# Bias stage of an attention-plus-mixing kernel: written issue order on SyncE, and the last bias stores moved behind the first head pair's tile loads

## The chip, the cores and the metric

The kernel runs on one core of one Trainium2 chip. The metric is the device time of one execution in microseconds (us). Before the change it was 751.64 us (median of 3 runs, 751.6 to 753.61).

## What is computed

The reference is attention with a learned relative-position bias, followed by a Fourier mixing and a dense layer. Only the attention matters here (4 batches, 8 heads, 576 positions, head width 64, 32 hidden units in the bias network):

```python
rel = (pos[:, None] - pos[None, :])
x = (log1p(abs(rel)) / log1p(maximum(pos[:, None], 1.0)))[..., None]
h = maximum(x @ w1 + b1, 0.0)
bias = h @ w2                                   # 576 x 576 x 8 heads
scores = q @ k.T / 8 + bias.transpose(2, 0, 1)
attn = softmax(scores); out = attn @ v
```

The bias does not depend on the batch. It is computed once, for all 8 heads, and then used by 16 units (4 head pairs by 4 batches).

## The kernel before

**Two stages matter.** The bias stage computes the bias of all heads, in 36 groups `u` of 16 query rows, 4 steps each (144 steps `n`). Each step makes one hidden tile on VectorE (DVE) or ScalarE (ACT), lines 390 and 392 (three of four on DVE), and two matmuls on TensorE (PE), line 412. When a group is done, `bias_evac` copies its PSUM tile to a ring of 4 slots of 4 groups each (line 358, ACT). The attention stage then goes through the 16 units; every unit has nine blocks of scores: S (matmuls, line 282), D (bias added and row maximum, DVE, line 303), X (exponential, ACT, line 318), then transposes T and products with v.

**Where the bias goes.** With every fourth group (`u` = 3, 7, ... 35) a ring slot is full: 64 query rows of 8 heads. Two transfers take heads 0 and 1 from the ring straight into the first head pair's bias tiles in SBUF (line 367; for `u` = 35 three transfers of `rest_bias`, lines 257 to 260). Two such slots fill one tile: `u` = 27 and 31 fill the fourth. Six more transfers, `keep_bias` (line 351), store heads 2 to 7 of the slot in a DRAM buffer `bias_d`, from which `load_bias` (line 249) fetches the tiles of the later head pairs. That is 54 stores, of 144 KB each, in nine groups of six. All of these, and the loads of q and k (line 199) and v (line 206), are issued on SyncE's queue (SP). The q and k of a unit are then split into high and low parts by `prep`: units 0 and 1 on ACT (line 217) and DVE (line 223), the later ones on GpSimd (POOL, lines 219 and 223).

**Some blocks of unit 0 run early.** When a tile of the first pair is complete, `first_scores` issues S, D and X of unit 0 for it. Block 6 of unit 0 (here called D6) is the first to use the fourth tile; it is written after the loop over the steps. The bias stage has one PSUM tile for such scores, so the next block of unit 0 (S7) has to wait for D6. The attention stage follows in the order that the list `SECOND` gives: `S1 S7' D1 D7' X7' S2 T00' ...` (a prime stands for unit 0, none for unit 1).

**What sets the order.** Inside a block of `manual_schedule` the named engines issue in written order. Everywhere else a planner sets the order when the program is built: on a simulated timeline every free engine takes, of the instructions that are ready, the one written first. In the attention stage PE, DVE and ACT are in such a block and SP is not; in the bias stage no engine is. So a store, or a load that is written much later, may stand on SP's queue wherever the planner found the queue free. On the chip each queue then works in the order given, and an issue that waits holds up all behind it.

Of the kernel before, what the change touches and what calls it, by code (L numbers as in the profile page):

```python
# [9 lines left out]
F32 = mybir.dt.float32  # L10
# [8 lines left out]
B, H, S, D = 4, 8, 576, 64  # L19
DM, FF, HID = 512, 2048, 32  # L20
P = 128
HP = H // 2
CH = S // 2
# [4 lines left out]
L0, L1, L2 = 0, 42, 64  # L28
WAIT = 24
EV = 40  # L30
AHEAD = 19
HB = {"d": 8, "a": 6}
WHO = "ddda"
# [104 lines left out]
def body(ctx, tc, a, out):  # L138
    nc = tc.nc
# [53 lines left out]
    def load(n):  # L193
        hp, b = units[n]
        t = []
        for nm, w in (("qT", 2 * S), ("kT", KW)):
            f = ldp.tile([P, w], F32, tag=nm, name=nm)
            for e in range(2):
                nc.sync.dma_start(f[64 * e:64 * e + 64], a[nm][hp, b])
            t.append(f)  # L200
        ld[n] = t

    def load_v(n):
        hp, b = units[n]
        v = vt[n] = vp.tile([P, 5, P], F32, tag="v", name="v")
        nc.sync.dma_start(v, a["v"][hp, b].rearrange("(t p) c -> p t c", p=P))

    def prep(n):
        q, k = ld.pop(n)
        qs = stp.tile([P, 2 * S], F32R, tag="qs", name="qs")  # L210
        kh = stp.tile([P, KW], F32R, tag="kh", name="kh")
        kl = stp.tile([P, KW], F32R, tag="kl", name="kl")
        stk[n] = (qs, kh, kl)

        def hi(dst, src, c):
            if n < 2:
                nc.scalar.activation(dst[:, c], src[:, c], AF.Copy)
            else:
                nc.gpsimd.tensor_scalar(dst[:, c], src[:, c], 1.0, 0.0, ALU.mult, ALU.add)  # L219

        def lo(dst, src, ref, rows, c):
            eng = nc.vector if n < 2 else nc.gpsimd
            eng.tensor_tensor(dst[rows, c], src[rows, c], ref[rows, c].bitcast(F32), ALU.subtract)  # L223

        every, low = slice(0, 128), slice(64, 128)
        ca, cb, ck = slice(0, S), slice(S, 2 * S), slice(S, KW)
        return [
            lambda: hi(qs, q, ca), lambda: lo(qs, q, qs, low, ca),
            lambda: hi(kh, k, ca), lambda: lo(kl, k, kh, every, ca),
            lambda: hi(qs, q, cb), lambda: lo(qs, q, qs, low, cb),  # L230
            lambda: hi(kh, k, ck), lambda: lo(kl, k, kh, every, ck),
        ]
# [82 lines left out]
    def expo(n, i):  # L315
        blk = (BLK if n else BLK0)[i]
        p = prob(n, blk)
        nc.scalar.activation(  # L318
            p, p, AF.Exp, bias=nms[n][:, blk:blk + 1], scale=-1.0, accum_out=sums[n][:, blk:blk + 1])

    def first_scores(i):
        scores(0, i)
        largest(0, i)
        expo(0, i)

    with ExitStack() as st:
        hpool = pool("hp", 1, stack=st)
        ring = xp.tile([P, 4, 4, S], F32, tag="x", name="ring")
        bps = pool("bps", 3, PSUM, stack=st)
        sps = pool("sps0", 1, PSUM, stack=st)  # L330

        sm = rawp.tile([P, 66 + 5 * NG], F32, tag="raw", name="sm")
        w1c, b1c, w2 = sm[:, 0:1], sm[:, 1:2], sm[:, 2:66].rearrange("p (r c) -> p r c", r=2)
        lt, inv = sm[:, 66:66 + 4 * NG], sm[:, 66 + 4 * NG:]
        nc.sync.dma_start(sm, a["sm"])
        parts = ((512, 1148), (0, 512), (1148, NT0 + S))
        for i, (c0, c1) in enumerate(parts):
            (nc.sync if i else nc.scalar).dma_start(tw[:, c0:c1], a["tab"][:, c0:c1])
        nc.scalar.activation(sqp.tile([P, 8], F32, tag="sq", name="first")[:, 0:1], ident[:, 0:1], AF.Relu)
        nc.vector.tensor_scalar(lt, lt, b1c, None, ALU.mult)  # L340
        for i, (c0, c1) in enumerate(parts):
            if i == 9:
                nc.scalar.activation(tw[:, c0:c1], tw[:, c0:c1], AF.Copy, scale=w1c)
            else:
                nc.vector.tensor_scalar(tw[:, c0:c1], tw[:, c0:c1], w1c, None, ALU.mult)

        def keep_bias():

            u, src = later.pop(0)
            for e in range(2, H):  # L350
                nc.sync.dma_start(bias_d[4 * (u - 3):4 * (u + 1), e], src[:, e])  # L351

        def bias_evac(u, ps):
            g = u % 4
            o = ring[:, u // 4 % 4]
            dst = o[:, g].rearrange("p (c s) -> p c s", c=2)
            if u % EV != EV - 1:
                nc.scalar.activation(dst, ps[:, :, :CH], AF.Copy, scale=inv[:, u:u + 1])
            else:
                nc.vector.tensor_scalar(dst, ps[:, :, :CH], inv[:, u:u + 1], None, ALU.mult)  # L360
            if g < 3:
                return
            r0 = 16 * (u - 3)
            src = o.rearrange("(r h) g s -> r h g s", h=H)
            for e in range(2):
                if r0 < 512:
                    nc.sync.dma_start(bt[0, r0 // 128][r0 % 128:r0 % 128 + 64, e], src[:, e])
                else:
                    rest_bias(bt[0, 4], e, src[:, e])
            later.append((u, src))  # L370
            if len(later) > 1:
                keep_bias()
            if u % 8 == 7:
                due.extend([(4 * u + WAIT, u // 8 * 2), (4 * u + WAIT + 2, u // 8 * 2 + 1)])

        pending, early, later = [], [], []
        due = []
        ps = None
        steps = bias_steps()
        ahead = {}  # L380

        def hidden(n):
            u, t4, _, low, _ = steps[n]
            col = lt[:, 4 * u + t4:4 * u + t4 + 1]
            off = NT0 if low is None else N0 - low
            src = tw[:, off:off + S]
            who = WHO[n % len(WHO)]
            h = hpool.tile([P, S], F32, tag="h" + who, name="h" + who, bufs=HB[who])
            if who == "a":
                nc.scalar.activation(h, src, AF.Relu, bias=col)  # L390
            else:
                nc.vector.tensor_scalar(h, src, col, 0.0, ALU.add, ALU.max)  # L392
            return h

        for n, (u, t4, rev, low, _) in enumerate(steps):
            for k in range(n, min(n + AHEAD, len(steps))):
                if k not in ahead and (k <= n + 2 or WHO[k % len(WHO)] != "d"):
                    ahead[k] = hidden(k)
            if n in (L0, L1):
                load(n // L1)  # L400
                load_v(n // L1)
            if n in (L0, L2):
                early.extend(prep(n // L2))
            if early and n % 2:
                early.pop(0)()
            while due and due[0][0] <= n:
                first_scores(due.pop(0)[1])
            h = ahead[n]
            if t4 == 0:
                ps = bps.tile([P, 2, 512], F32, tag="ps", name="bps")  # L410
            for c in range(2):
                nc.tensor.matmul(  # L412
                    ps[32 * t4:32 * t4 + 32, c, :CH], w2[:, int(rev)], h[:, c * CH:(c + 1) * CH],
                    start=True, stop=True, tile_position=(0, 32 * t4),
                )
            if t4 == 3:
                pending.append((u, ps))
            if t4 == 2 and len(pending) > 1:
                bias_evac(*pending.pop(0))
        for e in pending:  # L420
            bias_evac(*e)
        for _, i in due[:-1]:
            first_scores(i)


    with ExitStack() as st:
# [161 lines left out]
        for n in range(U - 1):  # L588
            pr = prep(n + 1) if n else []
            if n in WIDE:  # L590
                wd = weights(WIDE.index(n))
            between = {4 + 8 * i: [piece] for i, piece in enumerate(pr)}
            turn_of(n, between)
            if n + 2 < U:
                load(n + 2)
            if n == 0:
                while later:
                    keep_bias()
                x = xp.tile([P, B, 5, DM], F32, tag="x", name="x")
            if n == 14:  # L600
                fs = tabp.tile([P, 3, 2, 2, NK], F32R, tag="tab", name="fs")
                nc.gpsimd.tensor_copy(fs[0:1, 0, 0, 0, 0:1], vt[14][0:1, 0, 0:1])
                nc.gpsimd.dma_start(fs, a["fs"])
# [215 lines left out]
        n = U - 1  # L819
# [4 lines left out]
        ut, across, high, low = flip(un)  # L824
# [77 lines left out]
        for w in TAIL:  # L902
            u = n - w.count("'")
# [604 lines left out]
```

## Time and profile before

| what | value |
|---|---|
| median of 3 runs | 751.64 us |
| the profiled execution's own time | 752.28 us |
| its span, first to last instruction | 750.5 us |
| PE busy | 734.4 us (98% of the span), 4731 instructions |
| DVE / ACT / POOL busy | 489.1 / 442.0 / 346.8 us |
| DMA queue of SP and its share of 16 engines | 58976 packets, 102.13 MB, 48.1% |
| stores bias_d<-ring | 54 of 144.0 KB, 2.8 us from issue to landing (median) |

The profiled execution is 0.64 us above the median of the runs; 1.78 us of its time lie outside the span. A row of a timeline gives the start, the duration, the engine, the line, the operation and its tiles, the count, and in brackets the idle time of the engine before it with the event that ended it. SPq is the queue of SyncE. The granted clock of PE is 1.00 in every stretch.

### The profile page before, as it was taken

How to read it: one execution, taken by the hardware profiler on the slowest of the kernel's cores; microseconds unless marked ns; L12 is line 12 of the kernel's file. 1: busy time of each engine (PE TensorE's matmuls, PEld its weight loads, DVE VectorE, ACT ScalarE, POOL GpSimd, SP SyncE). 2: the span in 40 equal slices, each digit the busy share in tenths (PEclk: the TensorE clock that was granted, in tenths of full speed). 3: DMA queues.
4: the chain of work that ended last, by engine and by line, in shares of the span. 5: the costliest groups of instructions: out<-in, count | busy, mean ns of one | idle time of the engine just before them, and what ended most of it. 6: DMA issues, size and time to landing. Idle time of an engine off the chain costs nothing.

```text
span 750.5 us, 13327 instructions
## 1 busy us (share of the span) xinstructions
PE 734.4 (98%) x4731; PEld 604.9 (81%) x4731; DVE 489.1 (65%) x1044; ACT 442.0 (59%) x912; POOL 346.8 (46%) x301
## 2 busy tenths in 40 slices
PE   6999999999999999999999999999999999999998
PEld 4567888888878888878888888878878888888897
DVE  7997685888688788785665476656564444354443
ACT  7997888888888887844333344344433332244453
POOL 0002654565455664125554445366854453344442
PEclk9999999999999999999999999999999999999999
DMA  8988779669688992365422311211242123652432
GB/s 218 245 219 208 202 206 293 147 197 272 150 219 248 266 290 94 122 213 180 147 92 72 91 50 43 57 42 58 71 140 71 57 84 99 210 154 76 136 92 78
DMA packets 62771, 110.85 MB, mean 148 GB/s; under 512 B 9232, under 2 KB 28304, under 8 KB 61584
## 3 DMA queue, kind: packets, MB, share of 16 engines
q1 hardware_dynamic: 58976, 102.13, 48.1%
q10 hardware_dynamic: 3440, 4.78, 2.0%
q0 software_dynamic: 288, 3.08, 1.1%
q8 instruction: 37, 0.61, 0.4%
q14 instruction: 30, 0.25, 0.1%
HBM read 86.24 MB, written 21.07 MB: 143 GB/s over the span
## 4 chain that ended last, share of the span: by engine, by line
PE 89%; DMA 3%; ACT 2%; DVE 2%; SPq 1%; issue 1%; POOL 1%; DVEq 0%; ACTq 0%; POOLq 0%
PE acc L999 14%; PE hp L974 14%; PE acc L1249 12%; PE o L483 11%; PE s L282 11%; PE t L462 8%; PE hpy L1218 3%; PE hpx L1218 3%; PE hpa L1218 3%; PE zp L681 3%; PE abp L701 2%; PE bps L412 1%; PE hpb L1218 1%; DMA bias<-ring 1%; SPq L351 1%
## 5 line engine op out<-in xcount | busy, mean ns | idle before, releaser
L940 POOL TENSOR_TENSOR w2l<-w2f,w2h 128x512 fp32r<-128x512 f32 x64 | 84.9, 1328 | 92.0 <-ACT w2h L939 91.8
L940 POOL TENSOR_TENSOR w1l<-w,w1h 128x512 fp32r<-128x512 f32 x55 | 72.8, 1323 | 70.5 <-ACT w1h L939 68.2
L303 DVE CUSTOM_DVE_ANT_0 p<-s,bias 128x576 f32<-128x576 f32 x128 | 95.1, 753 | 12.8 <-PE s L282 8.7
L282 PE MATMUL s<-kh,qs 128*128 128x288 f32 (+1 forms) x320 | 100.7, 332 | 1.9 <-DVE nm L303 1.9
L442 ACT ACTIVATE pt<-t 128x512 f32<-128x512 f32 x141 | 80.6, 597 | 32.0 <-PE t L462 17.6
L318 ACT ACTIVATE p<-p,nm 128x576 f32<-128x576 f32 x128 | 98.3, 776 | 1.8 <-DVE nm L303 1.8
L282 PE MATMUL s<-kl,qs 128*128 128x288 f32 (+1 forms) x320 | 89.0, 294 | 0.9 <-DVE kl L223 0.9
L939 ACT ACTIVATE w2h<-w2f 128x512 fp32r<-128x512 f32 x80 | 50.2, 627 | 58.0 <-PE acc L999 21.4
L483 PE MATMUL o<-pt,v 128*64 128x288 f32 x640 | 81.4, 409 | 0.0
L462 PE MATMUL t<-ident,p 128*128 128x128 f32 x576 | 79.0, 273 | 0.6 <-ACT pt L442 0.6
L219 POOL TENSOR_SCALAR kh<-kT 128x576 fp32r<-128x576 f32 (+1 forms) x28 | 23.5, 856 | 119.0 <-PE s L282 80.1
L983 DVE SCALAR_TENSOR_TENSOR hl<-hp,hh 128x512 fp32r<-128x512 f32 (+1 forms) x48 | 28.9, 602 | 73.3 <-ACT hh L982 73.1
L939 ACT ACTIVATE w1h<-w 128x512 fp32r<-128x512 f32 x55 | 34.7, 631 | 65.8 <-PE hp L974 52.5
L483 PEld LDWEIGHTS o<-pt,v 128*64 128x64 f32 x640 | 44.4, 137 | 31.2 <-issue 2.7
L462 PEld LDWEIGHTS t<-ident,p 128*128 128x128 f32 x576 | 67.3, 140 | 1.7 <-ACT pt L442 1.3
L282 PEld LDWEIGHTS s<-kh,qs 128*128 128x128 f32 (+1 forms) x320 | 58.6, 183 | 6.7 <-DVE hd L392 2.3
L999 PE MATMUL acc<-w2l,hh 128*128 128x512 f32 x160 | 62.4, 391 | 0.0
L999 PE MATMUL acc<-w2h,hh 128*128 128x512 f32 x160 | 62.4, 393 | 0.0
L282 PEld LDWEIGHTS s<-kl,qs 128*128 128x128 f32 (+1 forms) x320 | 58.9, 184 | 1.2 <-DVE kl L223 1.2
L999 PE MATMUL acc<-w2h,hl 128*128 128x512 f32 x160 | 59.5, 391 | 0.0
L412 PE MATMUL bps<-hd,sm 128*32 128x288 f32 x432 | 52.1, 429 | 6.2 <-DVE hd L392 5.4
L1249 PE MATMUL acc<-w2h,hh 128*128 128x512 f32 x128 | 50.0, 391 | 0.0
(200 smaller groups left out, 1770.3 us busy)
## 6 DMA issues: line engine op xcount, KB each, us to landing
w2f<-w_d SPq DMA_DIRECT2D x80, 256.0 KB, 2.7
raw<-m SPq DMA_DIRECT2D x24, 512.0 KB, 5.4
w<-w_d SPq DMA_DIRECT2D x45, 256.0 KB, 3.2
kT<-kT SPq DMA_DIRECT2D x32, 304.0 KB, 4.7
qT<-qT SPq DMA_DIRECT2D x32, 288.0 KB, 6.1
bias_d<-ring SPq DMA_DIRECT2D x54, 144.0 KB, 2.8
bias<-bias_d SPq DMA_DIRECT2D x24, 288.0 KB, 5.6
v<-v SPq DMA_DIRECT2D x16, 320.0 KB, 7.6
```

Of the source, the lines that this page charges most:

```text
L282: nc.tensor.matmul(ps[:m, c, :CH], qs[:, c0:c0 + m], kk[:, k0 + c * CH:k0 + (c + 1) * CH], start=k == 0, stop=k == 1, skip_group_check=True)
L303: nc.vector.tensor_tensor_reduce(p, bank.pop((n, i))[:, :, :CH], bias, -0.125, 3.0e38, ALU.add, ALU.min, nms[n][:, blk:blk + 1])
L318: nc.scalar.activation(p, p, AF.Exp, bias=nms[n][:, blk:blk + 1], scale=-1.0, accum_out=sums[n][:, blk:blk + 1])
L442: nc.scalar.activation(dst, src, AF.Copy)
L462: nc.tensor.transpose(tp[:, 128 * t:128 * t + 128], pb[t].rearrange("p h s -> p (h s)")[:, k0:k0 + 128], ident)
L483: nc.tensor.matmul(os_[u][e, c, :CH], vt[u][:, j, e], pts[u][:, 2 * j + h if j < 4 else 8, c * CH:(c + 1) * CH], start=j == 0, stop=j == 4 ...
L939: nc.scalar.activation(h, src, AF.Copy)
L940: eng.tensor_tensor(l, src, h.bitcast(F32), ALU.subtract)
L974: nc.tensor.matmul(ps[:, :N], w[wi][:, P * kb:P * kb + P], ut[ui][:, kb, :N], start=i == 0, stop=i == len(mm) - 1)
L999: nc.tensor.matmul(acc[t], h[i][:, P * t:P * t + P], w[j], start=f == 0 and k == 0, stop=f == NF - 1 and k == 2)
L1218: nc.tensor.matmul(self.ps[bank], w[wi][:, P * kb:P * kb + P], u[ui][:, kb], start=first and k == 0, stop=k == len(mm) - 1, skip_group_che ...
L1249: nc.tensor.matmul(self.acc[t], h[i][:, P * t:P * t + P], w[j], start=f == 0 and k == 0, stop=f == NF - 1 and k == 2)
```

## The change

The loop over the 144 steps is put in a block that keeps SP (and SP alone) in written order. `keep_bias` takes the number of stores to issue, one by one, in place of a fixed group of six. It is called at every full slot: as before with the previous slot's six up to `u` = 23, then with none at `u` = 27, with four at `u` = 31, with all but six (fourteen) at `u` = 35, and with the last six after the load for unit 2.

```diff
-        def keep_bias():
-
-            u, src = later.pop(0)
-            for e in range(2, H):
+        def keep_bias(most):
+
+            for _ in range(most):
+                u, e, src = later.pop(0)
                 nc.sync.dma_start(bias_d[4 * (u - 3):4 * (u + 1), e], src[:, e])
...
-            later.append((u, src))
-            if len(later) > 1:
-                keep_bias()
+            later.extend([(u, e, src) for e in range(2, H)])
+            keep_bias({27: 0, 31: 4}.get(u, len(later) - 6))
...
-        for n, (u, t4, rev, low, _) in enumerate(steps):
...
-        for e in pending:
-            bias_evac(*e)
+        with tc.manual_schedule(engines={mybir.EngineType.SP}):
+            for n, (u, t4, rev, low, _) in enumerate(steps):
...
+            for e in pending:
+                bias_evac(*e)
         for _, i in due[:-1]:
             first_scores(i)
...
             if n + 2 < U:
                 load(n + 2)
             if n == 0:
-                while later:
-                    keep_bias()
+                keep_bias(len(later))
                 x = xp.tile([P, B, 5, DM], F32, tag="x", name="x")
```

The lines of the loop's body are the same, one level further in. What the loop writes for SP, in this order: at step 0 the load of q and k and the v of unit 0, at step 42 those of unit 1, and at every fourth group's `bias_evac` (which runs ten steps after the group's first step, at the end for the last two) the two tile loads and then the stores of the slot before.

## Rows read from the trace of the kernel before

**Rows 1.** Busy time by engine, two stretches (us), each with clock, DMA share, GB/s

```profile
4.03:63.41 59.38, 55.88 (x593) 33.72 (x595) 58.25 (x132) 55.80 (x90) 0.00 (x0) 1.00 0.89 228
80.00:750.00 670.00, 663.66 (x4027) 558.66 (x4025) 420.67 (x884) 373.59 (x796) 337.71 (x287) 1.00 0.47 138
```

**Rows 2.** Timeline of PE around the end of the bias stage

```profile
65.08 0.29 PE L282 MATMUL s<-kl,qs 128*128 128x288 f32 x1
66.42 0.40 PE L282 MATMUL s<-kh,qs 128*128 128x288 f32 x1 [1.06 <-DVE nm L303]
...
75.83 0.37 PE L282 MATMUL s<-kh,qs 128*128 128x288 f32 x1 [0.48 <-DVE nm L303]
```

**Rows 3.** Timeline of DVE in the bias stage

```profile
42.14 0.76 DVE L303 CUSTOM_DVE_ANT_0 p<-s,bias 128x576 f32<-128x576 f32 x1 [0.90 <-DMA bias<-ring]
...
57.32 6.09 DVE L392 TENSOR_SCALAR hd<-tw,sm 128x576 f32<-128x576 f32 x14
65.60 0.76 DVE L303 CUSTOM_DVE_ANT_0 p<-s,bias 128x576 f32<-128x576 f32 x1 [2.19 <-DMA bias<-ring]
```

**Rows 4.** Chain of waits that ended last: start, us, what

```profile
61.52 3.95 DMA bias<-ring
```

**Rows 5.** Timeline of ACT: first split of unit 1, ring copies of groups 31 and 35

```profile
18.40 1.26 ACT L217 ACTIVATE qs<-qT 128x576 fp32r<-128x576 f32 x2 [0.18 <-DMA qT<-qT]
...
60.39 0.74 ACT L358 ACTIVATE ring<-bps,sm 128x576 f32<-128x576 f32 x1 [0.50 <-PE bps L412]
...
64.70 0.74 ACT L358 ACTIVATE ring<-bps,sm 128x576 f32<-128x576 f32 x1 [0.55 <-PE bps L412]
```

**Rows 6.** Timeline of SP's queue: issues only

```profile
13.49 1.11 SPq L199 DMA_DIRECT2D qT<-qT  x2
...
24.76 1.22 SPq L367 DMA_DIRECT2D bias<-ring  x2
...
57.04 3.74 SPq L351 DMA_DIRECT2D bias_d<-ring  x6
60.83 0.59 SPq L249 DMA_DIRECT2D bias<-bias_d  x1
...
68.89 4.38 SPq L351 DMA_DIRECT2D bias_d<-ring  x7
...
77.11 0.55 SPq L199 DMA_DIRECT2D kT<-kT  x1
```

**Rows 7.** DMA issues between 48 and 61 us: count, KB, median us to landing

```profile
bias<-ring SPq DMA_DIRECT2D x4, 144.0 KB, 2.6
```

**Rows 8.** The same between 61 and 67 us

```profile
bias<-bias_d SPq DMA_DIRECT2D x1, 288.0 KB, 4.0
bias<-ring SPq DMA_DIRECT2D x2, 144.0 KB, 4.4
```

**Rows 9.** DMA issues of the whole run, from the page

```profile
kT<-kT SPq DMA_DIRECT2D x32, 304.0 KB, 4.7
```

**Rows 10.** Timeline of POOL: the split of unit 2, the start of unit 3's

```profile
71.14 1.38 POOL L219 TENSOR_SCALAR kh<-kT 128x576 fp32r<-128x576 f32 x2 [69.83 <-PE s L282]
...
76.79 2.80 POOL L223 TENSOR_TENSOR qs<-qT,qs 64x576 fp32r<-64x576 f32 x2
85.59 1.37 POOL L219 TENSOR_SCALAR kh<-kT 128x576 fp32r<-128x576 f32 x2 [6.00 <-DMA kT<-kT]
```

**Rows 11.** Timeline of PE: first scores of units 2 and 3

```profile
84.34 0.38 PE L282 MATMUL s<-kh,qs 128*128 128x288 f32 x1
...
99.59 0.38 PE L282 MATMUL s<-kh,qs 128*128 128x288 f32 x1
```

**Rows 12.** Timeline of DVE: first write of the tile x, which takes the ring's room

```profile
91.70 0.29 DVE L531 TENSOR_TENSOR x<-t,rr 128x128 f32<-128x128 f32 x1
```

**Rows 13.** Timeline of PE at a later manual block (L1249 inside it, L974 written after it)

```profile
693.70 0.28 PE L974 MATMUL hp<-uo,w1h 128*128 128x256 f32 x1
...
695.13 0.40 PE L1249 MATMUL acc<-w2l,hh 128*128 128x512 f32 x1
```

More of the change, by code (lines that the diff above doesn't have):

```diff
@@ L393, in hidden @@
             return h
-        for n, (u, t4, rev, low, _) in enumerate(steps):
[L396 to L419, printed above, removed]
@@ L420, in body @@
-        for e in pending:
-            bias_evac(*e)
+        with tc.manual_schedule(engines={mybir.EngineType.SP}):
+            for n, (u, t4, rev, low, _) in enumerate(steps):
+                for k in range(n, min(n + AHEAD, len(steps))):
+                    if k not in ahead and (k <= n + 2 or WHO[k % len(WHO)] != "d"):
+                        ahead[k] = hidden(k)
+                if n in (L0, L1):
+                    load(n // L1)
+                    load_v(n // L1)
+                if n in (L0, L2):
+                    early.extend(prep(n // L2))
+                if early and n % 2:
+                    early.pop(0)()
+                while due and due[0][0] <= n:
+                    first_scores(due.pop(0)[1])
+                h = ahead[n]
+                if t4 == 0:
+                    ps = bps.tile([P, 2, 512], F32, tag="ps", name="bps")
+                for c in range(2):
+                    nc.tensor.matmul(
+                        ps[32 * t4:32 * t4 + 32, c, :CH], w2[:, int(rev)], h[:, c * CH:(c + 1) * CH],
+                        start=True, stop=True, tile_position=(0, 32 * t4),
+                    )
+                if t4 == 3:
+                    pending.append((u, ps))
+                if t4 == 2 and len(pending) > 1:
+                    bias_evac(*pending.pop(0))
+            for e in pending:
+                bias_evac(*e)
```

## Prediction

> **What bounds the kernel now.** I read the busy time by stretch first. After 80 us PE is busy for 663.66 of 670.00 us [rows 1]: from there on PE is the bound, and what an earlier stage gains or loses on PE passes to the end undiminished. The bias stage, 4.03 to 63.41 us, is another matter: DVE is busy for 58.25 of 59.38 us, PE and ACT for about 55.8 each [rows 1]. So DVE's work sets that stage's length, and at most 59.38 - 58.25 = 1.1 us of it can be won without removing DVE work, of which this change removes none.
>
> Next come the timelines at the seam between the stages. PE ends the first score block of unit 1 at 65.08 + 0.29 = 65.37 us and starts the next, S7 of unit 0, only at 66.42, after 1.06 us in which it waited for DVE's row maximum [rows 2]. That is D6. DVE finished its last hidden tiles at 57.32 + 6.09 = 63.41 and then sat idle for 2.19 us before D6, until a transfer bias<-ring had landed [rows 3]. The chain of waits goes the same way: that transfer, the first of the two of group 31, took from 61.52 to 65.47 us [rows 4]. The last of its ring rows had been copied by ACT at 60.39 + 0.74 = 61.13 us [rows 5]. SP was then busy with one transfer for the second head pair, 60.83 to 61.42, and before that with six stores [rows 6]. The reader is to see a wait of four parts: DVE for a landing, the landing for its issue, the issue for SP, and PE for DVE; only the last, 1.06 us, is time of the kernel.
>
> **The change, part by part.**
>
> *Twelve stores move behind group 31's loads.* Before, the slots of groups 3 to 27, seven times six stores, were issued ahead of them; written order leaves those of groups 3 to 19, five times six. One store takes SP 3.74 / 6 = 0.62 us [rows 6], so 12 x 0.62 = 7.5 us of SP time and 12 x 144 KB leave the queue ahead of D6's rows. After the two loads of group 27 SP has nothing of its own to do until 61.13. The loads of group 31 can issue at about 61.2 in place of 61.52.
>
> How fast they land then is not shown, so I bound it. Low: 2.6 us, the median of four such loads between 48 and 61 us [rows 7]. High: the 3.95 us of the chain [rows 4], in a stretch where a 288 KB load issued 0.69 us ahead took 4.0 us and the two loads 4.4 [rows 6, 8]. A lower end would change nothing, since S7 cannot start before 65.37 in any case. The landing is at 63.8 or at 65.15, and D6, 0.76 us long [rows 3], ends at 64.6 or 65.9. PE can use S7's room from 65.37 on. By the low end all of the wait goes, 66.42 - 65.37 = 1.05 us; by the high end 0.4 us. Anything up to 3.3 us gives the whole. I take 2.6, because the rows of group 31 stand, like those four, behind no large load: 1.05 us gained. What is late next is ACT: it copies group 35 until 64.70 + 0.74 = 65.44 [rows 5], and D6's exponential follows it; before, DVE's wait hid that.
>
> The trace shows six stores ahead of a quick load [rows 7] and one big load ahead of a slow one [rows 8]. The Trainium skill ("DMA: Bandwidth & Descriptors", Queues, rings and completion order) says that each DMA engine consumes a ring in the order of issue. By that rule whatever stands ahead on SP's queue counts, store or load; with the next pair's load still ahead, the gain would be the 0.4 us of the high end. That is the second rival below.
>
> *Stores of the earlier groups come one group later.* Written order puts each slot's six behind the next slot's loads. A ring slot is written again four slots later, and the stores still end more than a group ahead of that; cost nothing. If SP fell back by a further group, ACT's ring copies would wait.
>
> *Unit 1's loads move.* Before, they were issued from 13.49 us [rows 6]. Now they are written behind the loads of group 7, issued at 24.76 to 25.98, and behind six stores: 25.98 + 3.7 = about 29.7. Their four issues and v then hold SP for some 5 x 0.6 = 3 us ahead of group 11's loads. Unit 1's first scores end at 65.37, so the data is in time. What moves is its split, four pieces on ACT of about 1.26 / 2 = 0.63 us [rows 5] and four on DVE, from around 20 us to 34 us or later. DVE's and ACT's sums stay. A new wait may arise: those engines work in order, and before ACT waited 0.18 us for q [rows 5]. Against that, DVE waited 0.90 us for a tile at 42.14 [rows 3], and stores where large loads stood may end that. I bound the sum of both by -0.9 (the wait goes) and +3 us (the issue time of SP's extra 3 us shows in full on DVE), and take 0, since the only row of such a wait for q is 0.18 us.
>
> *Twelve stores more come after 61 us.* Loads of group 31 until 62.4, four stores until 64.9, group 35's three transfers from its ring copy at 65.44 until 67.3, fourteen stores until 67.3 + 14 x 0.62 = 76.0, the last six until 79.7. Before, the stores were done at 68.89 + 4.38 = 73.27 [rows 6]. Behind them wait unit 3's k, issued at 77.11 before [rows 6], the raw weights, the small transfers for the row sums and the second pair's tiles. Unit 3's k comes up to 79.7 - 77.11 = 2.6 us later. POOL, which already idles 6.00 us for it until 85.59, would start at 88.2, and take as long as for unit 2, 76.79 + 2.80 - 71.14 = 8.45 us [rows 10], until 96.7; unit 3's first scores are at 99.59 [rows 11], 98.5 with the gain. Covered by 1.8 us. The tile x takes the ring's room and is first written at 91.70 [rows 12]; the last store lands near 79.7 + 2.6. Covered. Cost nothing, and if that cover is gone, the excess falls on PE in full.
>
> *Unit 2's loads* have to reach POOL by 71.14 [rows 10]. They are written behind the fourteen stores but need only the room that unit 1's split leaves free. Later, instructions written after a manual block do run within it: the L974 matmul at 693.70 stands ahead of L1249 ones [rows 13]. So I let the planner put these loads in SP's open gap, 56 to 61 us: cost nothing.
>
> **Sum.** -1.05 + 0 + 0 = -1.05 us, so the profiled execution of 752.28 would become 751.2. That execution is 0.64 us above the median of 751.64; against the median I predict 750.6.
>
> **The rivals.** A difference of about 0.3%, 2.25 us, is what a measurement of this kernel can tell from no change.
>
> *Forecast, chance 0.41:* D6's wait goes; 750.6, between 749.3 and 751.3.
>
> *The gap fills up, 0.22:* other heads' tiles and unit 2's loads, four of about 300 KB [rows 9], move into the gap ahead of group 31, which lands after 3.95 us as now. For it: the load at 60.83 [rows 6] stands there already. Against it: a gap of 5 us lets them go early. Gain 0.4 us: 751.2.
>
> *More than the seam, 0.20:* also the 0.90 us at 42.14 and the 0.48 us at 75.83 [rows 2, 3] go, and the stage ends earlier. 1.05 + 0.9 + 0.2 to 0.48 = 2.15 to 2.4, with all of DVE's idle 2.6: 749.0 to 749.5. For it: DVE bounds that stage. Against it: the same engine takes unit 1's split later.
>
> *Waits inside the bias stage, 0.10:* the split of unit 1 or D2 waits for SP's later loads, up to 3 us; net of the gain 0 to +2: 751.6 to 753.6.
>
> *Unit 2's loads come behind the stores, 0.07:* this ends on the other side. If they are not moved into the gap, they issue from 76.0 to 78.4, the last lands near 77.8 + 4.7 = 82.5 [rows 9], and POOL's 8.45 us end at 91.0. PE wants the result at 84.34 [rows 11]: 6.6 us slower, 758.2. It decides from a landing at 84.34 - 1.05 - 8.45 = 74.8 us on. Against it: [rows 13].
>
> **How the numbers follow.** Faster by more than 0.3%, below 749.4: most of the third case and the edge of the first, 0.22. Slower, above 753.9: the last case and a little of the fourth for a larger wait than I bounded, 0.10. Within: 0.68. The range starts at 748.9, so as to take in the third case, and ends at 753.3; it leaves out the last case and the worst of the fourth, with a margin for what a median of three can differ (one of the runs shown was 753.61). The forecast's own range is 749.3 to 751.3.
>
> **What would show it.** Right: DVE's idle before D6 falls from 2.19 us to below 0.5, group 31's first load lands within 3.3 us of an issue near 61.2, and PE's 1.06 us before S7 is gone; unit 2's q and k are issued between 40 and 61 us; POOL's wait for unit 3's k grows by no more than 2.6 us and no scores wait for POOL. Wrong: idle of ACT or DVE for q or k of unit 1 between 30 and 42 us, D2 idle for over 1 us, SP still busy at 61 us, or a PE wait at unit 2's or 3's first scores. The prediction fails as a whole if the order on SP before 61 us is not the written one.

## The result, and the profile after

The changed kernel takes 757.78 us (median of 10 runs, 756.19 to 761.13) against 753.16 us for the kernel before beside it (median of 10 runs, lowest 751.6): a ratio of 1.0071, 95% interval 1.0055 to 1.0088. The forecast was 750.6, a gain of 1.05; the change costs 4.6. (A few single runs far off the rest, here one of 4173.59 us, stand in the medians but not in the ratios.) The profiled execution is one of 757.78 us with a span of 756.0 (before 750.5), so its trace can be set against the prediction's own.

Where the 5.5 us of span were lost can be read from one row per unit, the first transpose of its probabilities on PE (line 456): from there on PE is the bound, as it was [rows 1]. After minus before it is 4.12 us at the first unit (78.14 against 74.02), 4.47 at the third, about 4.5 to 4.6 until 245 us, 5.49 from 262 us on. So three quarters of the loss is there before the first unit is finished. The last step, 0.9 us between 245 and 262 us, is not put down to the change: DVE waits there for a tile of the fourth head pair (0.51 us at 252.42), and a run of the kernel before (run 5 below) loses 0.85 us at the same unit, with a wait of 0.53. Busy time by stretch (the columns of rows 1), with the bias stage first:

```profile
4.03:66.70 62.67, 53.99 (x578) 31.84 (x579) 57.81 (x131) 54.90 (x89) 0.00 (x0) 0.97 0.77 197
54.60:57.96 3.36, 0.01 (x1) 0.00 (x0) 0.82 (x3) 1.39 (x4) 0.00 (x0) 1.00 0.79 213
58.00:59.00 1.00, 1.00 (x4) 0.87 (x4) 1.00 (x3) 0.81 (x2) 0.00 (x0) 0.54 0.89 220
80.00:750.00 670.00, 666.29 (x4048) 560.38 (x4048) 423.48 (x887) 376.31 (x804) 340.18 (x290) 1.00 0.49 141
```

DVE's work in the bias stage is what it was (57.81 us busy against 58.25), but the stage is 3.3 us longer: DVE now idles 4.9 us in place of 1.1. Between 54.60 and 57.96 almost everything stands still, PE with 0.01 us of work in 3.36. And behind that stop the clock granted to PE is 0.54, then 0.50, its lower level of 1.2 GHz, until about 61.5 us; the kernel before has 1.00 throughout the stage [rows 1]. The timeline of DVE says what it was waiting for:

```profile
39.81 1.49 DVE L223 TENSOR_TENSOR kl<-kT,kh 128x576 fp32r<-128x576 f32 x2
41.22 0.75 DVE L303 CUSTOM_DVE_ANT_0 p<-s,bias 128x576 f32<-128x576 f32 x1
...
46.01 6.96 DVE L391 TENSOR_SCALAR hd<-tw,sm 128x576 f32<-128x576 f32 x16
57.14 0.76 DVE L303 CUSTOM_DVE_ANT_0 p<-s,bias 128x576 f32<-128x576 f32 x1 [4.17 <-DMA bias<-ring]
...
66.85 0.76 DVE L303 CUSTOM_DVE_ANT_0 p<-s,bias 128x576 f32<-128x576 f32 x1
...
75.47 0.76 DVE L303 CUSTOM_DVE_ANT_0 pr<-s,bias_r 128x576 f32<-128x576 f32 x1 [2.03 <-DMA bias_r<-ring]
```

Read it against rows 3. The wait at 42.14 is gone (41.22 has none), and D6's 2.19 us are gone too (66.85 has none): the change does what it says. The last row, the block that needs group 35's rows, is taken up with run 8. But the row maximum at 57.14, the one for block 4 of the first unit, which needs group 23's rows and which I call D4 from here, waits 4.17 us. In the kernel before it waited for nothing:

```profile
52.53 0.74 DVE L303 CUSTOM_DVE_ANT_0 p<-s,bias 128x576 f32<-128x576 f32 x1
```

On PE the same, after and then before:

```profile
57.96 0.54 PE L282 MATMUL s<-kh,qs 128*128 128x288 f32 x1 [3.35 <-DVE nm L303]
70.86 0.40 PE L282 MATMUL s<-kh,qs 128*128 128x288 f32 x1 [0.34 <-DVE nm L303]
78.14 0.27 PE L456 MATMUL t<-ident,pr 128*128 128x128 f32 x1
```

```profile
74.02 0.27 PE L456 MATMUL t<-ident,pr 128*128 128x128 f32 x1
```

The 1.06 us before S7 [rows 2] are gone: S7 starts at 69.84, right behind S1. What is left at the seam is a new and smaller wait, 0.34 us at the block after it, S2, for D1. But PE stands 3.35 us some eight microseconds before S7's old place. Why group 23's rows were late is to be read on SP's queue, after first and then before:

```profile
27.22 1.18 SPq L199 DMA_DIRECT2D qT<-qT  x2
...
43.84 1.18 SPq L199 DMA_DIRECT2D qT<-qT  x2
...
50.56 0.54 SPq L199 DMA_DIRECT2D kT<-kT  x1
51.20 1.20 SPq L367 DMA_DIRECT2D bias<-ring  x2
...
71.97 12.60 SPq L351 DMA_DIRECT2D bias_d<-ring  x20
...
89.40 0.53 SPq L167 DMA_DIRECT2D raw<-m  x1
```

```profile
23.44 1.18 SPq L199 DMA_DIRECT2D qT<-qT  x2
...
35.81 1.18 SPq L199 DMA_DIRECT2D kT<-kT  x2
37.09 1.22 SPq L367 DMA_DIRECT2D bias<-ring  x2
...
49.03 1.19 SPq L367 DMA_DIRECT2D bias<-ring  x2
```

Before, unit 1 was loaded from 13.49 us [rows 6] and unit 2's q and k followed at 23.44 and 35.81, as soon as the split of unit 1 left the room. Now unit 1 is loaded from 27.22; its split on DVE ends at 41.30 (first row of the DVE fence); and so unit 2's q and k come at 43.84 and 50.56. Both kernels have a large load just ahead of a pair of bias rows. Before it stood ahead of group 15 (37.09), and the price was the 0.90 us of rows 3. Now it stands ahead of group 23, issued 2.2 us later than before (51.20 against 49.03), although the last ring copy of that group had ended at 48.75. The DMA issues of that moment (count, KB, median us to landing), after and then before, show the second half of the delay:

```profile
kT<-kT SPq DMA_DIRECT2D x1, 304.0 KB, 4.8
bias<-ring SPq DMA_DIRECT2D x2, 144.0 KB, 5.7
```

```profile
bias<-ring SPq DMA_DIRECT2D x2, 144.0 KB, 2.8
```

5.7 us to landing, where before the same pair took 2.8. Last, the chain of waits runs through three transfers:

```profile
51.20 5.81 DMA bias<-ring
...
68.44 6.12 DMA raw<-m
...
89.40 7.11 DMA raw<-m
```

The first is D4's. The second, 512 KB of raw weights (line 167; ACT, line 169, and DVE, lines 174 to 176, convert them during the units), stands ahead of group 35's rows, whose first load is issued at 70.10 and lands 4.7 us later. The third is a load of raw weights that used to go out by 74.5 us and now stands behind the twenty stores: ACT's first step on it waits 0.54 us and starts at 96.54, 4.8 us later than before.

### The profile page after: what moved, and what is told of

Its sections match the earlier page's. It is cut to its first block, busy times and chain, and to the rows that moved or that the text cites. A ratio compares the mean times of both kernels' runs of the same rounds, so it can differ in the third digit from the quotient of the medians.

```text
span 756.0 us, 13321 instructions
## 1 busy us (share of the span) xinstructions
PE 735.0 (97%) x4731; PEld 604.0 (80%) x4731; DVE 491.6 (65%) x1044; ACT 441.6 (58%) x912; POOL 346.3 (46%) x301
## 4 chain that ended last, share of the span: by engine, by line
PE 81%; DVE 6%; DMA 5%; issue 3%; SPq 2%; ACT 1%; POOL 1%; ACTq 0%; DVEq 0%; POOLq 0%
PE acc L998 14%; PE hp L973 14%; PE acc L1248 12%; PE o L483 9%; PE s L282 8%; PE t L462 6%; PE hpy L1217 3%; PE hpx L1217 3%; PE hpa L1217 3%; DVE hd L391 3%; PE zp L680 3%; DMA raw<-m 2%; PE abp L700 2%; PE hpb L1217 1%; SPq L351 1%
## 5 line engine op out<-in xcount | busy, mean ns | idle before, releaser
L219 POOL TENSOR_SCALAR kh<-kT 128x576 fp32r<-128x576 f32 (+1 forms) x28 | 21.2, 774 | 122.2 <-PE s L282 73.3
L998 PE MATMUL acc<-w2h,hh 128*128 128x512 f32 x160 | 62.7, 393 | 0.0
L412 PEld LDWEIGHTS bps<-hd,sm 128*32 128x32 f32 x432 | 27.9, 115 | 27.6 <-ACT ring L358 7.3
```

What stands on the lines that cost most here:

```text
L412: nc.tensor.matmul(ps[32 * t4:32 * t4 + 32, c, :CH], w2[:, int(rev)], h[:, c * CH:(c + 1) * CH], start=True, stop=True, tile_position=(0, ...
L998: nc.tensor.matmul(acc[t], h[i][:, P * t:P * t + P], w[j], start=f == 0 and k == 0, stop=f == NF - 1 and k == 2)
```

## The experiments

Theory after these readings: the loss is D4's wait, made by unit 1's late loads, which make SP late and draw unit 2's k in front of group 23. Rivals: the written order as such is slow, or holding stores back is.

**Run 1. The order alone**, no stores held back: `keep_bias({27: 0, 31: 4}.get(u, len(later) - 6))` becomes `keep_bias(len(later) - 6)`.

> Written order on SP with no holding back: at every full slot the previous slot's six stores are issued, as in the kernel before, and the last six after the loop. My theory (the loss is D4's wait for group 23's tile rows, because SP is late and unit 2's k stands just ahead of them) says that holding is not to blame: D4's wait stays near 4.2 us, the clock still falls to 0.5 after it, and the ratio to the kernel before stays at 1.005 to 1.008. Rival (the twelve held stores, which come later, cost the time): the ratio falls to 1.002 or less.

Measured: 755.87 us, ratio 1.0025 (0.9993 to 1.0056), profiled span 752.8.

```profile
55.77 0.76 DVE L303 CUSTOM_DVE_ANT_0 p<-s,bias 128x576 f32<-128x576 f32 x1 [1.70 <-DMA bias<-ring]
...
66.26 0.76 DVE L303 CUSTOM_DVE_ANT_0 p<-s,bias 128x576 f32<-128x576 f32 x1 [0.88 <-DMA bias<-ring]
```

D4's wait is there, but smaller (the rows landed in 4.5 us, with the same k ahead of them). PE waited 0.66 us, its clock did not fall, and the first transposes came 1.86 us later than before. The weights were not late. My theory had the wait stay near 4.2 us, and so missed; the rival is favoured, that part of the loss belongs to holding back. One profile does not show it: run 6 will find D4's wait at 2.42 us in the changed kernel itself.

**Run 2. Unit 2's loads put where nothing waits.** The change, with `load(2)` written behind group 27's loads.

> The changed kernel, with unit 2's q and k written in the block right behind group 27's tile loads, so that no part of them stands ahead of the loads of groups 19, 23 and 27. My theory: group 23's loads issue near 49.5 in place of 51.20 and land within 3.5 us in place of 5.8; D4's wait falls from 4.17 us to at most 1, the time by 3 to 4.5 us, to a ratio of 0.999 to 1.003. Rival (SP is late because of unit 1's loads and the stores in written order): the wait stays above 2.5 us and the ratio above 1.004.

Measured: 758.89 us, 1.0071 (1.0044 to 1.0098): the time expected was missed. With no large load ahead, group 23's rows landed in 3.2 us and D4's wait fell from 4.17 to 1.42. But group 31's rows now had unit 2's q and k and two tiles of the next pair in front, and D6's wait came back, dearer than before: the prediction's second rival, brought about by the edit. The first transposes came 3.12 us late; 3.5 us more were lost near 290 us, for a reason that run 3 shows.

```profile
53.56 0.76 DVE L303 CUSTOM_DVE_ANT_0 p<-s,bias 128x576 f32<-128x576 f32 x1 [1.42 <-DMA bias<-ring]
...
67.50 0.76 DVE L303 CUSTOM_DVE_ANT_0 p<-s,bias 128x576 f32<-128x576 f32 x1 [3.04 <-DMA bias<-ring]
```

**Run 3. Unit 1's loads put back early.** The change, with `L0, L1, L2 = 0, 16, 64` for `0, 42, 64`.

> The changed kernel, with unit 1's q, k and v written at step 16, ahead of group 3's tile loads, in place of step 42. Unit 2's loads stay free for the planner. My theory: the five issues (about 3.7 us of SP) leave the stretch from 27 to 31 us, where SP has just fallen behind, so group 23's loads issue when their ring rows are ready, and with unit 2's k moved ahead as well D4's wait goes below 0.5 us; ratio 0.998 to 1.001. Rival (D4's wait comes from written order of the stores as such): wait above 2 us, ratio above 1.004.

Measured: 760.65 us (four runs), 1.0088 (1.0054 to 1.0122): the time expected was missed widely, and yet the bias stage did as expected. Unit 2's loads were back at 23.21 and 36.64, D4 did not wait, D6 waited 0.25, and the first transposes started at 74.05, as in the kernel before.

```profile
53.23 0.74 DVE L303 CUSTOM_DVE_ANT_0 p<-s,bias 128x576 f32<-128x576 f32 x1
...
64.36 0.76 DVE L303 CUSTOM_DVE_ANT_0 p<-s,bias 128x576 f32<-128x576 f32 x1 [0.25 <-DMA bias<-ring]
```

The time went elsewhere: 0.9 us by the third unit, and then 4.8 us at once between 273 and 294 us. There GpSimd issues the load of the table fs (first row), and DVE's step on the weights that starts during that issue takes 6.24 us (second row); its usual time is 0.70.

```profile
266.71 0.74 POOL L602 DMA_DIRECT2D fs<-fs  x1 [0.36 <-POOL fs L601]
```

```profile
267.32 6.24 DVE L175 SCALAR_TENSOR_TENSOR raw<-raw 128x512 int32<-128x512 int32 x1
```

**Run 4. Both edits.**

> Both edits: unit 1's loads written at step 16 and unit 2's behind group 27's tile loads. My theory: no D4 wait, and D6's wait is gone too as in the changed kernel, so the time is below the kernel before by the 1 us of the seam: ratio 0.997 to 1.000. Rival (unit 2's loads at 27 slow group 31's tile loads): D6 waits over 1 us again and the ratio is 1.000 to 1.002.

Measured: 759.08 us, 1.0058 (1.0030 to 1.0086). D4 without a wait, D6 with 4.39 us for the reason of run 2, and again one long DVE instruction (5.82 us at 271.75, fs issued at 270.72).

**Runs 5 to 8. The spread taken out.** Runs 2, 3 and 4 all had such a long instruction in their profile, the kernels before and after had not. In all three it ended some 7 to 8 us after the start of the fs issue (7.97, 6.85, 6.85). Whether a step of the weights is caught depends on microseconds: in the kernel before, one began 0.34 us after the start of the issue (at 269.15) and was hardly longer than usual.

```profile
269.49 1.04 DVE L176 SCALAR_TENSOR_TENSOR uf<-uf,raw 128x512 int32<-128x512 int32 x1
```

So this may be what spreads the runs of every kernel here over 7 us. The test, and from here on part of every kernel, moves the issue to an earlier unit, away from the steps on the weights:

```diff
-            if n == 14:
+            if n == 9:
                 fs = tabp.tile([P, 3, 2, 2, NK], F32R, tag="tab", name="fs")
-                nc.gpsimd.tensor_copy(fs[0:1, 0, 0, 0, 0:1], vt[14][0:1, 0, 0:1])
+                nc.gpsimd.tensor_copy(fs[0:1, 0, 0, 0, 0:1], vt[9][0:1, 0, 0:1])
```

Run 5, in the kernel before ("control" from here on):

> The kernel before with one edit that has nothing to do with the change: GpSimd's load of the table fs (a single software-queue issue) is made in the turn without weights around 188 us in place of 269 us. Theory of the spread: runs of every kernel spread over some 7 us because this issue sometimes falls on one of DVE's integer instructions of the weights, which then takes 4 to 6 us in place of 0.7. Expected by it: no DVE instruction of lines 175 and 176 over 1.5 us, all runs within 1.5 us of each other, median 752.0. Rival (the spread has another cause): runs still spread from 751.5 to 758, median 754.5.

Measured: 751.93 us, nine of its ten runs within 751.2 to 753.87 (the tenth took 2541.67), no instruction of lines 175 and 176 over 1.25 us, where the kernel before had runs of 756 to 758.8 beside it. The theory of the spread holds for this kernel, a little looser than expected. It is not the whole of it: with fs early, run 7 still had one run of ten at 757.89, five us over its median, and run 8 ran from 755.98 to 760.21. Run 6, in the changed kernel:

> The kernel after with the same edit of fs, so that the cost of the change shows without that spread. Theory: the loss made in the bias stage and just behind it, 4.1 us at the first unit's transposes and about 0.4 us at the third's, stays; 752.0 + 4.5 to 5 = 756.7, runs within 1.5 us. Rival: part of the 4.6 us between the medians was the spread; then under 754.5.

Measured: 756.87 us, 754.96 to 757.77. So the change costs 4.94 us against its control: the loss is no accident of the spread. How it is divided differs from run to run. In this profile D4 waited 2.42 us, not 4.17 (the rows landed in 4.3 us in place of 5.7, in the same order on SP, issued at the same time):

```profile
55.52 0.76 DVE L303 CUSTOM_DVE_ANT_0 p<-s,bias 128x576 f32<-128x576 f32 x1 [2.42 <-DMA bias<-ring]
```

PE waited 1.63 us, its clock stayed at 1.00, and the first transposes were 2.18 us behind the kernel before instead of 4.12; 1.35 us were added by the fourth unit, around the late weights. Another 1.6 us came at the ninth unit, where DVE waited 1.94 us for a tile of the third head pair; whether the change has a part in that is not shown. And the seam's gain was not there: group 31's rows took 4.0 us to land, with two tiles of the second pair issued 1.7 us ahead of them, D6 waited 0.88 us, and PE 0.92 for the hidden tile behind D6. Run 7, the order without holding back, unit 1's loads early:

> The written order alone, without holding stores back, with the second unit's loads written where they stood before (step 16 in place of 42), and the edit of fs. Theory: the second unit's late loads are what made SP late for group 23's rows, so D4 (block 4 of the first unit) does not wait and the first unit's transposes start at 74.0 to 74.9 us; one tile of the second head pair still stands ahead of group 31's loads, so D6 waits 0.5 to 1.5 us; twelve stores behind group 35 are too few to delay the raw weights. Time that of the control with the same edit of fs, 752.0 within 0.8 us. Rival: written order by itself is slow (SP waits at each group's copies in turn); then D4 still waits over 1 us, the transposes start at 75.5 us or later, 753.5 or more.

Measured: 752.68 us, 0.75 over the control. D4 did not wait, D6 waited 1.98 (expected 0.5 to 1.5), the weights were on time. The rival "the written order is slow by itself" is worth about 0.75 us by these medians, with runs that overlap. Run 8, the stores held back, none behind group 27, twelve behind group 31 and twelve behind group 35, unit 1's loads early:

> As the run before it, and the stores held back: none behind group 27, twelve behind group 31, twelve behind group 35 (the change had four and twenty). Theory: with SP on time D6's wait goes as was forecast for the change (0.3 us or less left, against two tiles of the second pair issued ahead), D4 does not wait, and the raw weights are not late behind twenty stores: transposes at 73.6 to 74.1 us and no later loss by 100 us; 751.5, 0 to 1 us under the control. Rival: twelve stores more at 62 to 70 us delay group 35's rows or the raw weights; then the block of group 35 waits over 1 us, or the transposes of the third unit lose 0.5 us or more against the second's, 752.5 or more.

Measured: 757.58 us. D6's wait was 0.23 as expected, but the rival of this run came true: behind twelve stores, group 35's rows were issued 5 us after their last ring copy (70.42 against 65.37), and the block of that group (D8) waited. PE stood 3.39 us for it, and its clock fell to 0.5.

```profile
73.91 0.76 DVE L303 CUSTOM_DVE_ANT_0 pr<-s,bias_r 128x576 f32<-128x576 f32 x1 [5.19 <-DMA bias_r<-ring]
```

The changed kernel's 2.03 us at D8, 0.24 on PE, are of another kind. There the four stores held nothing up (last ring copy until 70.07, rows issued at 70.10), but the load of raw weights stood just ahead, and the rows took 4.7 us to land. In run 6, with the same four stores and that load 3.2 us ahead, they took 2.4.

**Runs 9 and 10. The change again, two ways.** Run 9 is run 3 with fs early:

> The change whole (order and holding, four stores behind group 31 and twenty behind group 35), only the second unit's loads written where they stood before (step 16), with fs early. Theory: D4 does not wait; D6 waits 0.3 us or less; the first unit's transposes start at 74.0 to 74.3 us; 0.5 to 0.9 us are lost by 101 us to the raw weights late behind the twenty stores; against the control with fs early +0.5 to +1.2 us, so 752.4 to 753.2, a ratio under 1.000 to the kernel before with its spread. Rival (the first run with these loads early was slow for a cause of its own, 760.65, not for the long DVE instruction): 756 or more also with fs early.

Measured: 755.42 us, 3.55 over the control measured beside it (751.87, run 11). The rival is out, though by little: without the long instruction the kernel came down from 760.65; but I had expected 0.5 to 1.2 over the control. D4 did not wait, and D6 waited 0.27. D8 waited 2.73 us, however. The timeline names PE's transposes as what ended it; but what landed just then were the last of group 35's rows, issued behind a load of raw weights, as the chain of waits has it:

```profile
68.48 3.31 DMA bias_r<-ring
```

PE stood 0.94 us for D8, and the first transposes came at 74.61, 0.59 behind the kernel before. The larger part of the excess is later, where the weights come late: DVE's last step on them ends at 102.4 us, a copy of the transposes stands behind it, and PE waits for that copy. From the third to the fourth unit this run loses 1.1 us.

```profile
100.61 1.80 DVE L176 SCALAR_TENSOR_TENSOR uf<-uf,raw 128x512 int32<-128x512 int32 x1
102.34 0.45 DVE L444 COPY pt<-t 64x64 f32<-64x64 f32 x2
```

```profile
102.94 0.63 PE L452 MATMUL t<-ident,pr 128*128 128x128 f32 x4 [0.31 <-DVE pt L444]
```

The lag in this profile ends at 1.9 us, less than the medians differ by; where the rest is lost is not shown.

Run 10, the change with fs early and unit 2's q and k between group 31's loads and group 35's:

> The change whole, but the third unit's q and k written behind group 31's loads and four stores, ahead of group 35's, with fs early: no large load stands ahead of group 23's or group 31's rows. Theory: group 23's rows land within 3.5 us of their issue near 50.3 (with k ahead 4.3 to 5.8), D4 waits 1 to 2 us in place of 2.4 to 4.2, what is left being SP's lag of the second unit's loads; D6 waits 0.5 us or less; first transposes at 75.0 to 76.0. The price appears at group 35's rows, behind four large loads and four stores: they land 4.5 to 6 us after their issue, D8 waits 2 to 4 us; total 754.5 to 756.5. Rival (k ahead is not what makes group 23 slow): landing 4.5 us or more and D4's wait 2.5 us or more.

Measured: 759.38 us, 3 us above what I expected. Group 23 landed in 3.1 us, D4 waited 0.39 and D6 0.60: with the large load away, D4's wait is gone even with unit 1's loads late. The price at D8 was larger than I had put it:

```profile
75.98 0.76 DVE L303 CUSTOM_DVE_ANT_0 pr<-s,bias_r 128x576 f32<-128x576 f32 x1 [6.39 <-DMA bias_r<-ring]
```

**Run 11. The control once more,** as the version that beats both kernels.

> The kernel before with fs early once more, with more rounds, as the version that beats both. Theory of the spread: all runs between 751.2 and 754, median 751.9, 0.15 to 0.3% under the kernel before, whose runs reach 758; no DVE instruction of lines 175 and 176 over 2 us. Rival: runs of 756 and more appear here too, ratio 0.9995 or more.

Measured: 751.87 us (751.1 to 754.76, 12 runs), ratio 0.9981 (0.9964 to 0.9999) to the kernel before. It beats both, the kernel before by little, and its highest run is 754.76, where the kernel before reached 757.67 beside it.

**Run 12. The last corner of a square:** run 1 with fs early.

> The fourth corner of a square whose sides are holding back (yes, no) and the second unit's loads (step 42, step 16), all with the written order and fs early. Medians so far: held back and late 756.87, held back and early 755.42, not held back and early 752.68; control in planned order 751.9. Theory (the two costs are mostly separate: D4's wait belongs to the late loads, the late raw weights to holding back): 752.68 + (756.87 - 755.42) to + 2.2 = 754.1 to 754.9, D4 waits 1 to 2.5 us, no wait for the raw weights between 86 and 101 us. Rival (holding back is what makes the late loads dear, by leaving SP's gap open for large loads): 753.2 or less, D4's wait under 0.7 us.

Measured: 754.57 us (ratio 1.0024, 1.0005 to 1.0044), inside what was expected; D4 waited 1.89 us, and the weights were on time. One of its twelve runs took 820.87. With that the change is taken apart, all with fs early, medians in us over the control's 751.9:

| written order, and | unit 1's loads at step 16 | at step 42 |
|---|---|---|
| stores not held back | 752.68 (+0.8) | 754.57 (+2.7) |
| held back as in the change | 755.42 (+3.5) | 756.87 (+5.0) |

Loading unit 1 late costs 1.5 to 1.9 us, holding the stores back 2.3 to 2.7, the order itself 0.8. They add up within 0.4 us, less than single runs differ by, so neither is shown to make the other dear. (The medians come from three series of runs on two chips; the control had 751.93 and 751.87 in two of them.)

## Why the prediction was wrong

The change was forecast as -1.05 us and is +4.6, or +4.9 with the spread taken out. The seam was read rightly; three terms that stood at nothing were not nothing.

*Twelve stores behind group 31's loads: right, in its place, with some luck.* DVE's 2.19 us before D6 went to 0, PE's wait of 1.06 before S7 went, the 0.34 for D1 came, and group 31's rows landed 2.6 us after their issue, the value that I took. The lag behind the kernel before falls over the seam from 4.63 us at unit 1's first block (69.20 against 64.57) to 3.76 at its next (70.86 against 67.10): 0.87 us gained, close to the 1.05. The luck is that D4's stop had put the ring copies off: the rows could be issued only at 64.25, three us behind the second pair's tiles. Where the copies came earlier, in run 6, the tiles were close ahead and D6 waited 0.88 us. With unit 1's loads early (runs 3, 8 and 9) the tiles went 5 us ahead and D6 waited 0.23 to 0.27.

*Unit 1's loads, "take 0": the step that failed.* The bounds, -0.9 to +3, held the 1.5 to 1.9 us that the square gives it, by luck, since the upper one stood for SP's issue time showing on DVE; and the lower one was even seen: D2's wait did go. But the only wait I looked for on the dear side was the split's own for q (0.60 us on ACT in the changed kernel's trace, and harmless). I did not ask which block would next need rows behind the moved work. It was D4, whose rows were issued 2.2 us late.

*Unit 2's loads, "in SP's open gap, cost nothing": the same failure, one move further.* I wrote that they need only the room that unit 1's split leaves free, and then let them go anywhere. Their rows in the trace before (23.44 and 35.81 us) follow unit 1's split, which I was moving by 14 us. They followed it, to 43.84 and 50.56, and k took its place in front of group 23, at 1.3 to 2.9 us of landing: 4.1 to 5.7 us with it ahead (5.7 in the change, 4.5, 4.3 and 4.1 in runs 1, 6 and 12), 2.5 to 3.2 without (the kernel before and all other runs). Run 10 is the plainest: unit 1's loads late as in the change, only unit 2's loads away, and D4's wait was 0.39 us. The second rival had just this mechanism, the large load ahead of a pair of rows, priced well enough, and put it at group 31. The prediction drew there on the Trainium skill ("DMA: Bandwidth & Descriptors", Queues, rings and completion order), which says that each DMA engine consumes a ring in its order. The trace agrees for large loads ahead, by these landings. My own sign of being right, unit 2's q and k issued between 40 and 61 us, came true (43.84, 50.56 and 57.38) and was the harm.

*The stop and the clock.* A stop of PE can have a second price, which no bound of mine held: after the 3.35 us the granted clock lay near 0.5 for about 3.5 us. It fell to that level after stops of 1.92 us (run 2), 2.48 and 4.58 (run 10), 2.98 (run 4) and 3.39 (run 8) as well, and stayed at 1.00 after 1.63 (run 6) and after 2.05 (the change, at 38.98); a length of stop at which it falls does not come out of these runs. What it cost in the change is small as far as the rows show: DVE, which sets that stage's length, waited 0.44 us for PE's matmuls at 65.90. With the long stop the first transposes were 4.12 us late, with the shorter one of run 6 2.18.

*Twelve stores more after 61 us, "cost nothing": 2.3 to 2.7 us by the square.* I named four things that wait behind the stores, and looked up the due time of one of them, unit 3's k (and of the tile x); there POOL's wait grew from 6.00 to 8.98 us and no scores waited. The raw weights were in the same sentence, without a due time: before, they went out by 74.5 us, and ACT used them at 91.77. Behind twenty stores the load goes out at 89.40 and takes 7.11 us to land: ACT waits, and DVE's integer steps fall on the unit's transposes. Run 9 against run 7, and run 6 against run 12, lose 1.3 us more between the first and the fourth unit's transposes; the change's own profile lost 0.36. Another load of raw weights went out early, into the room that the stores had left, just ahead of group 35's rows. These then took 4.0 us and more to land (4.7 in the change), against 2.4 to 2.6 without, and D8 waited 2.03 us in the change and 2.73 in run 9, which cost PE 0.24 and 0.94. What makes up the rest of the 2.3 to 2.7 us is not settled: up to the fourth unit the pairs of profiles show 1.4 us (runs 7 and 9) and 1.9 us (runs 12 and 6), and the medians more.

*The chances.* "Waits inside the bias stage", which in kind is what came, though at D4 and not at the split or D2, had 0.10, since I summed its bounds against a single wait for q. Slower by over 0.3% had 0.10 as well. The range ended at 753.3 because D4 and the weights were in none of its ends. The median that I started from, 751.64, was also the low end of a spread over 7 us; beside the changed kernel the same one gave 753.16.

## What to carry to other kernels

When a load is moved, list what its buffer hands on: the next load into that room moves by as much, and lands in front of something else. And when work is put behind a due transfer, look up the due time of every other transfer that shares the queue behind it: a gain at the one that waits now is given back at the first that you did not look up. Before comparing versions within one per cent, look for what spreads the runs of a single kernel; here a single issue by GpSimd moved a profiled run by 3.5 to 5 us, as much as the change did.

## What was not expected of the hardware

One software-queue issue on GpSimd, 0.74 us long in the trace, kept a DVE integer instruction for 3.94, 6.24 and 5.82 us in three profiles, each ending some 7 to 8 us after the start of the issue. The one that began 0.34 us after that start, in the kernel before, took 1.04 us, and all others of these instructions stayed under 2 us. The long ones read two operands from SBUF. The Trainium skill ("SBUF — State Buffer", Who interferes with whom) says that a DVE instruction with two SBUF inputs and a GpSimd instruction that reads SBUF share a port, and that the later of them is blocked. The runs agree in kind as far as one engine held the other up; that the port is the cause is not shown here, and the rule alone would not give the 0.34 us case. That the hold outlasts the record of the issue by some 6 to 7 us is shown by these rows alone.
